# Attention phases that each hold one more pair of score tiles over, with the stack loads awaited at value products and some small work moved to other places

## The chip, the cores and the metric

The kernel runs on one core of a Trainium2 chip. The metric is the device time of one execution in microseconds (us), from three runs of the kernel before: median 1293.32, lowest 1293.25, highest 1293.84. One more execution was taken with the hardware profiler. It took 1295.3 us, of which 1293.3 are the span from the first to the last instruction of the core, and 2.0 lie around the span. All durations below come from that profiled execution.

## What is computed

Two blocks work on the same input `x` (2048 tokens, 512 channels), and a gate mixes them. Cut to what matters:

```python
qkv = x @ wqkv                       # 32 heads of 16 channels
scores = einsum("bhqd,bhkd->bhqk", q, k) * 16 ** -0.5
a = einsum("bhqk,bhkd->bhqd", softmax(scores), v) ... @ wo
h = layernorm(x)
u = gelu(einsum("bsd,sf->bdf", h, w1) + b1)      # mixes along tokens, F = 1792
b = transpose(einsum("bdf,fs->bds", u, w2) + b2)
out = g * a + (1 - g) * b            # g = sigmoid(sum(x * gate_w))
```

Products that need full precision are made of a high and a low part of each factor (three matmuls for one).

## The kernel before, in words

The first 305 us make `v`, `q`, `k` and the first mixer layer. What the change touches is the attention, from 305 us to 1274 us, and a tail of some 20 us behind it.

**Groups and phases.** Attention is cut into 32 groups: 2 halves of the queries by 16 pairs of heads. A group has 4 phases, and the 128 phases are numbered p0 to p127 (p = 4 x group + ph, the loop at L835). In each phase:

- PE (TensorE) makes 16 score tiles of 128x512 (L907) from the group's stacks `ks` (keys) and `qs` (queries). Scores use 64 rows of the array, so that a matmul of the dense work (L916, tile `dn`) runs in the other 64 rows at the same time. The dense work is the second mixer layer in p0 to p91 (14 a phase); there is none in p92 to p95; and it is the output projection in p96 to p127 (12 a phase, then 6, then 8).
- ACT (ScalarE) takes exponentials: six score tiles singly (L928), three pairs of tiles as 128x1024 (L869), and four tiles as one 128x2048 (L939) that DVE (VectorE) has copied out of PSUM before (L924, tile `pe`).
- PE multiplies the exponentials with `v` in `apply_v` (L792): each pair of score tiles takes 8 matmuls of 128x256, in four column groups of 32 that run side by side. They add up in one PSUM bank, `av`, which DVE then copies or adds into the group's sums `ot` in SBUF (L814, L816).

**What a phase holds over.** Two pairs (`HELD`, the four evacuated tiles) are multiplied with `v` one phase later, because their exponential comes last. The last of the other six pairs is held over too where a test in the code allows it (`whole`: both query blocks of a head must be covered, because the sums are kept by column halves). Up to p91 that is so in every phase. In the steady phases from p96 on it fails in half of the phases: there a phase has 56, 64 or 72 value products instead of 64 each.

**Loads and stores.** SP issues DMAs from one queue, in program order. In ph0 of each group it loads the query stacks of the next group (`load_q`, 8 DMAs), in ph1 the key stack (`load_k`, 6 DMAs, L505). The group that has just ended stores its sums in ph0 (8 DMAs: L781 to `o`, L783 to `r`, the sums of exponentials). Nothing waits for the stacks until the next group's first scores use them.

**Turned sums.** After every fourth group, `invert` (L613 to L625) loads `r` (tile `inv`, L617), takes maximum and reciprocal on DVE (L620, L621) and writes it back (L625, `ri`). For the two last blocks of the second half, DVE's part comes in the same phase as the load (p113 and p125), for the others two phases later. `fetch_o` and `fetch_half` (L635 to L650) then load `o` and `ri` again, and DVE multiplies and splits them (L949) for the output projection.

**Order.** The program is written out in the order of each engine; engines run their own instructions in that order. Work that other parts of the kernel want in a phase is put in a table: `call(p, ...)` runs at the start of phase p, ahead of the stack loads of that phase; `on_dve(p, ...)` runs on DVE behind the phase's evacuations and ahead of its sum.

**The tail.** Behind p127, the output projection of the last 8 row tiles is finished on PE: `others` (L996) makes those of the 12 matmuls of each tile that the dense work of the phases has not made.

Of the kernel before, what the change touches and what calls it, by code (L numbers as in the profile page):

```python
# [9 lines left out]
F32 = mybir.dt.float32  # L10
# [5 lines left out]
AX = mybir.AxisListType  # L16
SYNC = mybir.DependencyInfo(mybir.DependencyClass.Sync, mybir.DependencyReason.DATA)
REASON = "the two halves of the rows add to one bank"
PSUM = bass.MemoryType.PSUM
DRAM = bass.MemoryType.DRAM  # L20

P = 128
# [8 lines left out]
NB = 512  # L31
# [27 lines left out]
def gated_mix(ctx: ExitStack, tc: tile.TileContext, a_x, a_wqkv, a_wo, b_w1, b_b1, b_w2, b_b2, gate_w, out):  # L59
# [437 lines left out]


    def stack(dst, src, which, pair, cols, planes):
        b, r0 = divmod(pair * 2 * DH, P)  # L500
        for i in range(2):
            rows = slice(r0 + i * DH, r0 + (i + 1) * DH)
            for row, *part in planes:
                at = slice(i * HALF + row, i * HALF + row + DH)
                nc.sync.dma_start(dst[at].bitcast(F32), src[b][part[which], rows, cols])  # L505

# [58 lines left out]
    def call(at, *what):  # L565
        calls.setdefault(at, []).append(what)
# [14 lines left out]
    def open_end():  # L581

        nonlocal end, sums_of
        u_ctx.close()
        wk_ctx.close()
        end = end_ctx.enter_context(tc.tile_pool(name="end", bufs=1, side="right", reuse_waits="tile"))

        sums_of = end.tile([P, P], F32, name="sums_of")
        nc.vector.tensor_copy(
            sums_of.rearrange("p (j r) -> p j r", r=32),  # L590
            ident.rearrange("p (j r) -> p j r", r=32)[:, :, DH:VC].broadcast_to([P, P // 32, 32]),
        )
        least.append(end.tile([P, 1], F32, name="least"))
# [190 lines left out]

    def apply_v(av, grp, pairs, final=False):

        for n, pair in enumerate(pairs):
            for i, c, qb, pt in sorted(pair, key=lambda u: u[2]):
                for h in range(2):
                    j = 2 * qb + h  # L790
                    v_at = (c * H + grp % NP * 2 + i) * VC
                    nc.tensor.matmul(  # L792
                        av[32 * j : 32 * (j + 1), i * QC : (i + 1) * QC],
                        v_flat[:, v_at : v_at + 32],
                        pt[:, h * QC : (h + 1) * QC],
                        start=n == 0,
                        stop=n == len(pairs) - 1,
                    )
        covered = [{qb for pair in pairs for i, _, qb, _ in pair if i == n} for n in range(2)]
        assert all(len(c) != 1 for c in covered)  # L800
        if grp not in sums:
            sums[grp] = ot_pool.tile([P, NB], F32, name="ot"), [False, False]
        ot, begun = sums[grp]
        halves = [n for n in range(2) if covered[n]]
        if grp == NG - 1 and final:
            parts = [(x, y, True) for x, y in zip(column_halves(ot), column_halves(av))]
        elif len(halves) == 2 and begun[0] == begun[1]:
            parts = [(ot, av, begun[0])]
# [3 lines left out]
        for x, y, more in parts:  # L812
            if more:
                nc.vector.tensor_tensor(x, y, x, ALU.add)  # L814
            else:
                nc.vector.tensor_copy(x, y)  # L816
        for n in halves:
            begun[n] = True
        if final and grp < NG - 1:
            store(grp, sums.pop(grp)[0])  # L820

    engines = {getattr(mybir.EngineType, name) for name in ("PE", "Activation", "DVE", "Pool", "SP")}
    with tc.manual_schedule(engines=engines):
        kt, qt = {0: load_k(0)}, {0: load_q(0)}
        held, fence, turn, spare = [], None, 0, 0

        for n, (step, *args) in enumerate(first):
# [7 lines left out]
        for p in range(LAST + 1):  # L835
            grp, ph = divmod(p, PHASES)
            second = ph % 2
            for what, *args in calls.get(p, ()):
                what(*args)
            if ph == 0:  # L840
                at = [[0, 0], [0, 0]]
                if grp + 1 < NG:
                    qt[grp + 1] = load_q(grp + 1)
            if ph == 1 and grp + 1 < NG:
                kt[grp + 1] = load_k(grp + 1)
            if not second:
                beside = [step(*args) for step, *args in dense.get(p // 2, ())]
# [12 lines left out]

            swap = ph == PHASES - 1 and p < LAST and head[TWO[1][0]] == head[TWO[1][1]]
            order = [*TURNS[:4], TURNS[5], TURNS[4]] if swap else TURNS
# [79 lines left out]
            if p == 0:  # L942
                shift_rows(nc.vector, k_bufs[1])
            if second:
# [7 lines left out]
            spare = share[2]  # L952
            if ph < PHASES - 1 or swap:

                def whole(pairs):
                    met = {(i, qb) for pair in pairs for i, _, qb, _ in pair}
                    return all(len([1 for i, _ in met if i == n]) != 1 for n in range(2))

                if whole(turns[:-1] + (held if ph else [])):
                    now_held = now_held + turns[-1:]  # L960
                    turns = turns[:-1]
            if ph == 0:
                if held:
                    apply_v(av, grp - 1, held, final=True)
                    spare = share[3]
                    av = psum.tile([P, NB], F32, name=f"s{spare}")
                apply_v(av, grp, turns)
            elif p < LAST:
                apply_v(av, grp, held + turns)
            else:  # L970
                ot = sums[grp][0]
# [168 lines left out]
```

## Time and profile before

| what | value |
|---|---|
| median of three runs | 1293.32 us |
| profiled execution / its span | 1295.3 us / 1293.3 us |
| PE busy | 1280.4 us, 99% |
| ACT busy | 1091.3 us, 84% (9 tenths and more in each slice of the attention) |
| DVE busy | 671.0 us, 52% |
| GpSimd (POOL) busy | 180.0 us, 14% |
| granted TensorE clock, mean | 0.997 |
| DMA | 133.20 MB, 101 GB/s of HBM traffic over the span |

A busy PE in this table is one that has matmuls in its pipeline. It is not yet one that could go no faster: the ends of matmuls are modelled, and a matmul that starts late because of a wait is hardly seen in that share. How long a phase takes is better seen from the starts of its weight loads (PEld), which the trace records one by one. The first score of a phase is the first row of L907 behind the last row of L792.

### The profile page before, as it was taken

What the parts mean: (1) busy time and instruction counts of PE and PEld (TensorE: products, weight loads), DVE (VectorE), ACT (ScalarE), POOL (GpSimd) and SP (SyncE); (2) the same over time, 40 slices, a digit from 0 to 9 for tenths busy, and PEclk for the clock granted to TensorE, in tenths of its full rate; (3) what the DMA queues carried; (4) which work ended last, traced back from release to release, by engine and by line L of the source; (5) the groups of instructions that cost most, each with busy time, mean ns of one, the idle gap of its engine ahead of it and who ended that gap; (6) DMA issues with size and microseconds to landing.
All of it is one profiled execution on the core that took longest, in us unless ns stands there. A gap on an engine that the chain in (4) does not pass through costs nothing.

```text
span 1293.3 us, 33067 instructions
## 1 busy us (share of the span) xinstructions
PE 1280.4 (99%) x13278; PEld 850.4 (66%) x13278; DVE 671.0 (52%) x1155; ACT 1091.3 (84%) x1537; POOL 180.0 (14%) x272
## 2 busy tenths in 40 slices
PE   9999999999999999999999999999999999999997
PEld 7888888886666666666666666666665565655555
DVE  5675362438445545544544444454454665645555
ACT  3443343447999999999999999999999999999994
POOL 0210244553110111011011101101110000000000
PEclk9999999999999999999999999999999999999999
DMA  4497643327343343333334443333333654335411
GB/s 131 139 317 276 222 121 98 98 78 159 67 88 75 68 97 83 77 68 81 77 60 98 83 77 66 81 75 60 88 68 75 151 135 114 81 84 108 80 44 72
DMA packets 93581, 133.20 MB, mean 103 GB/s; under 512 B 16277, under 2 KB 55339, under 8 KB 90348
## 3 DMA queue, kind: packets, MB, share of 16 engines
q1 hardware_dynamic: 92844, 129.94, 41.2%
q8 instruction: 108, 1.77, 0.6%
q10 hardware_dynamic: 576, 1.05, 0.2%
q14 instruction: 53, 0.43, 0.1%
HBM read 97.00 MB, written 33.93 MB: 101 GB/s over the span
## 4 chain that ended last, share of the span: by engine, by line
PE 93%; ACT 4%; DVE 1%; issue 1%; DVEq 0%; ACTq 0%
PE av L792 28%; PE s L907 19%; PE acc L416 12%; PE t L907 10%; PE acc L73 10%; PE dn L916 6%; PE s L792 5%; ACT p L928 1%; ACT p L869 1%; ACT pe L939 1%; PE pa L996 1%; DVE pe L924 1%; PE acc L187 1%; PE dn L831 1%; PE acc L254 0%
## 5 line engine op out<-in xcount | busy, mean ns | idle before, releaser
L928 ACT ACTIVATE p<-s 128x512 f32<-128x512 f32 x768 | 395.7, 648 | 6.1 <-PE s L907 3.6
L869 ACT ACTIVATE p<-t 128x1024 f32<-128x1024 f32 x352 | 348.4, 1131 | 0.0
L907 PE MATMUL s<-qs,ks 64*128 64x512 f32 x1344 | 343.0, 404 | 1.1 <-DVE pe L924 0.7
L924 DVE COPY pe<-s 128x512 f32<-128x512 f32 x512 | 317.8, 683 | 6.9 <-PE s L907 6.4
L907 PEld LDWEIGHTS s<-qs,ks 64*128 64x128 f32 x1344 | 232.9, 184 | 97.5 <-issue 52.4
L792 PE MATMUL av<-p,v 128*32 128x256 f32 x4872 | 285.4, 379 | 0.0
L814 DVE TENSOR_TENSOR ot<-av,ot 128x512 f32<-128x512 f32 (+1 forms) x128 | 73.5, 575 | 396.6 <-PE av L792 396.6
L939 ACT ACTIVATE pe<-pe 128x2048 f32<-128x2048 f32 x129 | 259.5, 2014 | 0.0
L792 PEld LDWEIGHTS av<-p,v 128*32 128x32 f32 x4872 | 158.4, 110 | 104.9 <-issue 0.7
L907 PE MATMUL t<-qs,ks 64*128 64x512 f32 x704 | 185.1, 445 | 2.9 <-ACT p L928 0.4
L916 PE MATMUL dn<-u_lo,w_hi 64*128 64x512 f32 x430 | 174.1, 405 | 0.0
L916 PE MATMUL dn<-u_hi,w_lo 64*128 64x512 f32 x430 | 173.9, 404 | 0.0
L916 PE MATMUL dn<-u_hi,w_hi 64*128 64x512 f32 x428 | 173.2, 405 | 0.0
L66 POOL TENSOR_TENSOR w_lo<-w_raw,w_hi 128x512 fp32r<-128x512 f32 (+1 forms) x126 | 149.0, 1189 | 124.6 <-ACT w_hi L65 108.5
L907 PEld LDWEIGHTS t<-qs,ks 64*128 64x128 f32 x704 | 96.2, 184 | 83.4 <-ACT p L928 74.9
L792 PE MATMUL av<-pe,v 128*32 128x256 f32 x2048 | 138.1, 387 | 0.1
L920 POOL MEMSET token<- 1x1 f32 x124 | 12.7, 102 | 866.9 <-PE dn L916 811.2
L65 ACT CAST w_hi<-w_raw 128x512 fp32r<-128x512 f32 (+1 forms) x67 | 38.1, 569 | 79.2 <-PE acc L416 58.8
L792 PEld LDWEIGHTS av<-pe,v 128*32 128x32 f32 x2048 | 53.6, 109 | 54.2 <-ACT p L928 25.3
L416 PE MATMUL acc<-h_hi,w_hi 128*128 128x512 f32 x224 | 87.1, 389 | 0.0
L416 PE MATMUL acc<-h_lo,w_hi 128*128 128x512 f32 x224 | 87.1, 389 | 0.0
L416 PE MATMUL acc<-h_hi,w_lo 128*128 128x512 f32 x224 | 87.1, 389 | 0.0
(151 smaller groups left out, 1507.2 us busy)
## 6 DMA issues: line engine op xcount, KB each, us to landing
w_raw<-in_B_w_dram SPq DMA_DIRECT2D x96, 256.0 KB
ks<-kp SPq DMA_DIRECT2D x192, 128.0 KB
qs<-qp SPq DMA_DIRECT2D x256, 64.0 KB
qp<-pc SPq DMA_DIRECT2D x16, 768.0 KB
x<-in_A_x_dram SPq DMA_DIRECT2D x32, 256.0 KB
kp<-pc SPq DMA_DIRECT2D x16, 512.0 KB
w_raw<-in_B_w_dram SPq DMA_DIRECT2D x32, 128.0 KB
bp<-row SPq DMA_DIRECT2D x16, 256.0 KB
```

The costliest lines, as they stand in the source:

```text
L65: copy(hi, src)
L66: return sub(lo, src, hi.bitcast(F32), ALU.subtract)
L73: nc.tensor.matmul(ps, a, b, start=start and n == 0, stop=stop and n == last)
L416: nc.tensor.matmul(p, a, b, start=first and k == 0, stop=last and k == 2)
L792: nc.tensor.matmul(av[32 * j : 32 * (j + 1), i * QC : (i + 1) * QC], v_flat[:, v_at : v_at + 32], pt[:, h * QC : (h + 1) * QC], start=n == ...
L814: nc.vector.tensor_tensor(x, y, x, ALU.add)
L869: nc.scalar.activation(pt, twos[low, low + 1], AF.Exp, scale=SCALE)
L907: nc.tensor.matmul(s, kt[grp][rows_i, c * P : (c + 1) * P], qt[grp][rows_i, qb * NB : (qb + 1) * NB], start=True, stop=True,)
L916: mm = nc.tensor.matmul(ps, a[half], b[half], start=begin and not second, stop=last and bool(second))
L924: nc.vector.tensor_copy(pt, s)
L928: nc.scalar.activation(pt, s, AF.Exp, scale=SCALE)
L939: nc.scalar.activation(x, x, AF.Exp, scale=SCALE)
```

## The change

1. **Holding over.** Every phase but p127 holds its last pair of scores over. The test `whole` is gone, so that a phase has 64 value products throughout (p0 and p127 apart). For this the sums must be added by quarters: `ot` is set to zero by GpSimd at the start of each group (L844 of the new kernel) and DVE only adds, to the whole bank, to column halves, or to a quarter of 64x256.
2. **Awaiting at products.** `stack` notes each DMA that it issues; the value products of ph3 behind the first pair of tiles each wait for one of them (`await_loads`), in place of the next group's first scores.
3. **Loads ahead.** `load_q` and `load_k` are issued ahead of what the table calls in the same phase: `invert`, `fetch_o`, `fetch_half`, `load_wo`, the rows of `bp`.
4. **Constants and others.** The small constants (`sums_of`, `least`) are made in p101 in place of p92. In p0, the second key buffer's constant rows are set by GpSimd in place of DVE. A subtraction for the output projection moves from p115 to p116. One output tile (the one at p116 and p117) has 6 of its 12 matmuls in the phases in place of 8.

The core of the diff:

```diff
+    landed = []
     def stack(dst, src, which, pair, cols, planes):
...
-                nc.sync.dma_start(dst[at].bitcast(F32), src[b][part[which], rows, cols])
+                landed.append(nc.sync.dma_start(dst[at].bitcast(F32), src[b][part[which], rows, cols]))
...
     call(p0, open_end)
+    on_dve(p0 + 9, end_constants)
...
-    call(p2, fetch_o, 1, 2, (0, 1), (p2 + 1, p2 + 1, p2 + 1))
+    call(p2, fetch_o, 1, 2, (0, 1), (p2 + 1, p2 + 1, p2 + 2))
...
-        at = put_output(t, 6 if 2 * at < p2 + 2 else 8, at)
+        at = put_output(t, 6 if 2 * at < p2 + 3 else 8, at)
...
+                    if await_loads and n and landed:
+                        tc.add_manual_dep(mm.ins, landed.pop(0).ins.name, SYNC, reason=AHEAD_OF_USE)
...
+        if grp == NG - 1 and final:
+            parts = list(zip(column_halves(ot), column_halves(av)))
+        elif len(met) == 4:
+            parts = [(ot, av)]
         else:
-            cols = [slice(n * QC, (n + 1) * QC) for n in range(2)]
-            parts = [(ot[:, cols[n]], av[:, cols[n]], begun[n]) for n in halves]
+            at = [(every, cols[i]) for i in range(2) if {(i, 0), (i, 1)} <= met]
+            at += [(rows[qb], cols[i]) for i, qb in sorted(met) if (i, 1 - qb) not in met]
+            parts = [(ot[r, c], av[r, c]) for r, c in at]
+        for x, y in parts:
+            nc.vector.tensor_tensor(x, y, x, ALU.add)
...
-            for what, *args in calls.get(p, ()):
-                what(*args)
             if ph == 0:
+                sums[grp] = ot_pool.tile([P, NB], F32, name="ot")
+                nc.gpsimd.memset(sums[grp], 0.0)
...
             if ph == 1 and grp + 1 < NG:
                 kt[grp + 1] = load_k(grp + 1)
+            for what, *args in calls.get(p, ()):
+                what(*args)
...
-                shift_rows(nc.vector, k_bufs[1])
+                shift_rows(nc.gpsimd, k_bufs[1])
...
-            if ph < PHASES - 1 or swap:
...
-                if whole(turns[:-1] + (held if ph else [])):
-                    now_held = now_held + turns[-1:]
-                    turns = turns[:-1]
+            if p < LAST:
+                now_held = now_held + turns[-1:]
+                turns = turns[:-1]
...
-                apply_v(av, grp, held + turns)
+                apply_v(av, grp, held + turns, await_loads=ph == PHASES - 1)
```

**PE at the boundary of two groups.** The 15th and 16th score of p20 (tile `t3`, from `qs` and `ks1` of group 5) and the first value products behind them, before:

```order
L907 MATMUL t3_5303<-qs_4740,ks1_2704 128x512 [waits DVE_49,Activation_49]
L907 MATMUL t3_5303<-qs_4740,ks1_2704 128x512 [waits DMAHW6_49,DMAHW5_49,DMAHW4_49]
L792 MATMUL av_5302<-pe_5113,v_91 32x256 [waits Activation_49]
L792 MATMUL av_5302<-pe_5113,v_91 32x256 x7
L792 MATMUL av_5302<-p2_5186,v_91 32x256 x4
```

And now, value products of p19 (from the fifth on), one phase ahead:

```order
L799 MATMUL av_5167<-pe_5001,v_91 32x256 x3
L799 MATMUL av_5167<-pe_5001,v_91 32x256 [waits DMAHW6_49]
L799 MATMUL av_5167<-pe_5001,v_91 32x256 [waits DMAHW7_49]
L799 MATMUL av_5167<-pe_5001,v_91 32x256 [waits DMAHW0_49]
L799 MATMUL av_5167<-pe_5001,v_91 32x256 [waits DMAHW1_49]
L799 MATMUL av_5167<-p2_5074,v_91 32x256 [waits DMAHW2_49]
L799 MATMUL av_5167<-p2_5074,v_91 32x256 [waits DMAHW3_49]
```

The waits for DMA queues (DMAHW) have left the 16th score, which now has none, and fourteen value products of p19 wait for one each (six are shown). An instruction with three waits needs further instructions on PE's sequencer that wait ahead of it; one with a single wait holds it itself.

**SP in p112 and p113 (group 28).** The end of group 27's stores (`o12`, `r12`), the load of the turned sums (`inv`), the next key stack (`ks1`) and the way back (`ri12`), before:

```order
L781 DMA o12_2714<-ot_16057 16x2x256 [waits DMAHW3_49]
L783 DMA r12_2722<-ot_16057 2x1x256 [waits DMAHW4_49]
L617 DMA inv_16520<-r12_2722 128x64 [waits DMAHW5_49,DMAHW4_49,DMAHW6_49,DMAHW2_49,DMAHW0_49]
L505 DMA ks1_2704<-kp3_68 16x2048
L505 DMA ks1_2704<-kp3_68 16x2048 [waits DMAHW7_49]
L505 DMA ks1_2704<-kp3_68 16x2048
L505 DMA ks1_2704<-kp3_68 16x2048 [waits DMAHW1_49]
L505 DMA ks1_2704<-kp3_68 16x2048
L505 DMA ks1_2704<-kp3_68 16x2048 [waits DMAHW3_49]
L625 DMA ri12_2730<-inv_16520 128x64 [waits DVE_49]
```

And now:

```order
L788 DMA o12_2714<-ot_15933 16x2x256 [waits DMAHW3_49]
L790 DMA r12_2722<-ot_15933 2x1x256 [waits DMAHW4_49]
L508 DMA ks1_2704<-kp3_68 16x2048 [waits DMAHW5_49]
L508 DMA ks1_2704<-kp3_68 16x2048 [waits DMAHW6_49]
L508 DMA ks1_2704<-kp3_68 16x2048 [waits DMAHW7_49]
L508 DMA ks1_2704<-kp3_68 16x2048 [waits DMAHW0_49]
L508 DMA ks1_2704<-kp3_68 16x2048 [waits DMAHW1_49]
L508 DMA ks1_2704<-kp3_68 16x2048 [waits DMAHW2_49]
L623 DMA inv_16541<-r12_2722 128x64 [waits DMAHW4_49,DMAHW3_49]
L631 DMA ri12_2730<-inv_16541 128x64 [waits DVE_49]
```

The load of `inv` has gone from ahead of the six key loads to behind them; the write of `ri12` follows it at once.

**DVE in p113 and at the start of p114.** The same instructions stand in the same order before and now. Now (L626 and L627 are the maximum and the reciprocal, L821 the sum of p113, L930 the evacuations of p114):

```order
L930 COPY pe_16543<-s1_16579 128x512 [waits PE_49]
L676 SCALAR_TENSOR_TENSOR base8_16185<-dn_16419,g_77,base8_16185 128x512 [waits DMAHW2_49]
L626 TENSOR_SCALAR inv_16541<-inv_16541 128x64 [waits DMAHW3_49]
L627 RECIPROCAL inv_16541<-inv_16541 128x64 [waits DVE_49]
L821 TENSOR_TENSOR ot_16406<-av_16594,ot_16406 128x512 [waits PE_49]
L930 COPY pe_16657<-s4_16665 128x512 [waits PE_49,Activation_49]
```

Nothing has moved on this engine here. The instruction that waits for `inv` stands ahead of the sum of p113 and of the four evacuations of p114.

More of the change, by code (lines that the diff above doesn't have):

```diff
@@ L17 @@
 SYNC = mybir.DependencyInfo(mybir.DependencyClass.Sync, mybir.DependencyReason.DATA)
+AHEAD_OF_USE = "the next group's scores find their stacks awaited"
 REASON = "the two halves of the rows add to one bank"
@@ L588, in open_end, with end_constants @@
         sums_of = end.tile([P, P], F32, name="sums_of")
+        least.append(end.tile([P, 1], F32, name="least"))
+    def end_constants():
         nc.vector.tensor_copy(
@@ L592, in open_end @@
         )
-        least.append(end.tile([P, 1], F32, name="least"))
         nc.vector.tensor_reduce(least[0], ident.rearrange("p (j r) -> p j r", r=32)[:, :, DH], axis=AX.X, op=ALU.add)
@@ L791, in apply_v @@
                     v_at = (c * H + grp % NP * 2 + i) * VC
-                    nc.tensor.matmul(
+                    mm = nc.tensor.matmul(
                         av[32 * j : 32 * (j + 1), i * QC : (i + 1) * QC],
@@ L825, in gated_mix @@
         held, fence, turn, spare = [], None, 0, 0
+        landed.clear()
         for n, (step, *args) in enumerate(first):
@@ L859, in gated_mix @@
                     turn = 1 - turn
-            swap = ph == PHASES - 1 and p < LAST and head[TWO[1][0]] == head[TWO[1][1]]
+            swap = ph == PHASES - 1 and p < LAST and n_b == NSC - 2
             order = [*TURNS[:4], TURNS[5], TURNS[4]] if swap else TURNS
```

29 lines of the change are left out of this document (7 added, 22 removed).

## The prediction

> **What bounds the kernel now.** I read the page's shares first, then the starts of the phases in the weight loads of the timeline, then the phases that stand out.
>
> ```profile
> PE 1280.4 (99%) x13278; PEld 850.4 (66%) x13278; DVE 671.0 (52%) x1155; ACT 1091.3 (84%) x1537; POOL 180.0 (14%) x272
> ...
> L792 PE MATMUL av<-p,v 128*32 128x256 f32 x4872 | 285.4, 379 | 0.0
> ```
>
> PE seems to be all there is. But the share counts pipelines, and a late matmul hides in it. The rows of the weight loads (start, duration, operation, idle before) tell more. Here are p55 (ph3) and p56 (ph0), from first score to first score, and the six single exponentials of ACT in p55:
>
> ```profile
> 719.37 0.18 PEld L907 LDWEIGHTS s<-qs,ks 64*128 64x128 f32 x1 [0.41 <-issue]
> ...
> 722.81 0.21 PEld L907 LDWEIGHTS t<-qs,ks 64*128 64x128 f32 x2 [0.27 <-ACT p L928]
> 723.27 0.59 PEld L792 LDWEIGHTS av<-pe,v 128*32 128x32 f32 x16 [0.25 <-ACT p L928]
> ...
> 726.86 0.18 PEld L907 LDWEIGHTS s<-qs,ks 64*128 64x128 f32 x1 [0.41 <-issue]
> ...
> 730.31 0.42 PEld L907 LDWEIGHTS t<-qs,ks 64*128 64x128 f32 x2 [0.27 <-ACT p L928]
> 730.97 0.59 PEld L792 LDWEIGHTS av<-pe,v 128*32 128x32 f32 x16 [0.24 <-issue]
> ...
> 734.56 0.18 PEld L907 LDWEIGHTS s<-qs,ks 64*128 64x128 f32 x1 [0.41 <-issue]
> ```
> ```profile
> 719.90 3.09 ACT L928 ACTIVATE p<-s 128x512 f32<-128x512 f32 x6
> ```
>
> p55 takes 726.86 - 719.37 = 7.49 us: 3.90 of scores (to 723.27) and 3.59 of value products. The products start when the sixth single exponential lets a bank go, and the exponentials wait for the scores: PE and ACT bound the phase in one loop. ACT alone has little less to do. Phases without dense work, below, run at 7.39 and 7.40. So nothing large is to be had per phase; the change can only take away excesses over 7.49. p56 has one: its products start 4.11 behind its start, 0.21 late, and the pair of last scores spans 0.42 in place of 0.21.
>
> Now the long stretches: the starts of p4, p92, p93, p94 and p127.
>
> ```profile
> 335.36 0.18 PEld L907 LDWEIGHTS s<-qs,ks 64*128 64x128 f32 x1 [0.41 <-issue]
> ...
> 997.96 0.30 PEld L907 LDWEIGHTS s<-qs,ks 64*128 64x128 f32 x4 [0.41 <-issue]
> ...
> 1007.62 0.30 PEld L907 LDWEIGHTS s<-qs,ks 64*128 64x128 f32 x4 [0.41 <-issue]
> ...
> 1015.01 0.19 PEld L907 LDWEIGHTS s<-qs,ks 64*128 64x128 f32 x2 [0.41 <-issue]
> ...
> 1264.67 0.18 PEld L907 LDWEIGHTS s<-qs,ks 64*128 64x128 f32 x1 [0.41 <-issue]
> ```
>
> **Term 1, stacks awaited at products.** p4 to p91 are 88 phases in 997.96 - 335.36 = 662.60 us; 88 x 7.49 would be 659.12. The excess, 3.5 us, lies in the 22 phases that begin a group, as in p56: the 16th score waits for three or four DMA queues, and each wait beyond those that a matmul can hold is an instruction of its own on PE. Four waits cost 0.21 (p56); for three I estimate half, so 11 x 0.21 + 11 x 0.10 = 3.4. With the waits moved to products of ph3, each holding one, these instructions go: **-3.4**. What the awaited product costs is not seen before, since no product waits for a DMA there. Products that wait for ACT stand in the row of L792 with 0.0 idle: lower end nothing. Upper end: each like one of the waits of its own, 0.21 / 2 = 0.105, times 14 products in 31 groups, 434 x 0.105 = 45.6 us. I take nothing, the row of the same instruction; the data landed many us earlier (loads are issued in ph0 and ph1, awaited in ph3).
>
> **Term 2, p1.** DVE sets constant rows (L492) into p1 and begins the phase's sum late. The starts of p1 and p2, then DVE and ACT:
>
> ```profile
> 312.04 0.18 PEld L907 LDWEIGHTS s<-qs,ks 64*128 64x128 f32 x1 [0.41 <-ACT p L869]
> ...
> 320.38 0.18 PEld L907 LDWEIGHTS s<-qs,ks 64*128 64x128 f32 x1 [0.41 <-issue]
> ```
> ```profile
> 311.60 1.76 DVE L492 MEMSET ks<- 16x2048 f32 x1 [0.46 <-issue]
> 313.40 0.42 DVE L816 COPY ot<-av 128x256 f32<-128x256 f32 x1
> ...
> 313.23 3.09 ACT L928 ACTIVATE p<-s 128x512 f32<-128x512 f32 x6
> ```
>
> p1 takes 8.34; its DVE sum starts 1.36 behind the start, where 0.14 is usual (p114, term 5). So 1.2 of lateness cost 0.85. With GpSimd doing it, ACT remains late: its first exponential is 1.19 behind p1's start, against 0.53 in p55. I keep 0.65 of the 0.85: **-0.2** (-0.85 at the best). GpSimd's memsets, this one and one of 128x512 in each group, lie beside its idle time (14% busy): what uses the result comes half a phase later or more. No row shows them on GpSimd; if a group's first sum did wait, it would be for some part of DVE's 1.76, once a group.
>
> **Term 3, from p92 on.** p92 takes 9.66, because DVE makes the constants ahead of its evacuations, and then the clock falls:
>
> ```profile
> 997.90:1002.30 4.40, 3.69 (x20) 1.66 (x16) 3.60 (x9) 4.40 (x9) 0.00 (x0) 1.00 0.84 196
> 1002.30:1007.60 5.30, 5.30 (x66) 2.44 (x64) 0.42 (x1) 4.01 (x4) 0.00 (x0) 0.68 0.42 87
> ```
>
> (Columns: window, length, busy of PE, weight loads, DVE, ACT, GpSimd, granted clock, DMA share, GB/s.) If the low clock is a half, 0.68 over 5.30 means 3.4 us at half: the 3.59 of products took the 5.3 of this window, 1.7 more. That is a stage with 16 scores and no dense matmuls, prolonged by DVE. Moved to p101, the constants (0.6 us of DVE) lie where DVE, 52% busy, waits for products anyway; without that cover p102 would lose the 0.6. p92 should then look like p93: 1015.01 - 1007.62 = 7.39.
>
> From p95 on, a phase of 72 products is longer by a pair's 3.59 / 8 = 0.45, and one of 56 shorter by as much; but there ACT falls behind, and the next phase gives most of it back. With 64 throughout each phase takes 7.49. So p92 to p126 take 4 x 7.40 + 31 x 7.49 = 261.8, against 1264.67 - 997.96 = 266.7: **-4.9**. This includes the 0.77 that p116 loses before:
>
> ```profile
> 1181.42 0.18 PEld L907 LDWEIGHTS s<-qs,ks 64*128 64x128 f32 x1 [0.41 <-issue]
> ...
> 1189.23 0.18 PEld L907 LDWEIGHTS s<-qs,ks 64*128 64x128 f32 x1 [0.41 <-issue]
> ```
> ```profile
> 1181.28 1.23 DVE L949 TENSOR_TENSOR e<-o_sum,e 128x1024 fp32r<-128x1024 f32 x1
> 1182.42 0.68 DVE L814 TENSOR_TENSOR ot<-av,ot 128x512 f32<-128x512 f32 x1
> ```
>
> p116 has 56 products and should take 7.49 - 0.45 = 7.04; it takes 7.81. DVE's sum, 0.86 later than usual, holds the evacuations behind it and the scores that need their banks. The subtraction of 1.23 now comes a phase later. So a late sum costs a phase its lateness less 0.1 to 0.35 (0.86 gives 0.77, 1.2 gives 0.85).
>
> **Term 4, the tail.** One tile leaves two more matmuls to L996, behind p127, where PE alone sets the end:
>
> ```profile
> 1274.08 0.39 PE L996 MATMUL pa<-wo_lo,e 128*128 128x512 f32 x1
> 1274.31 0.39 PE L996 MATMUL pa<-wo_hi,e 128*128 128x512 f32 x1
> ```
>
> One each 0.23: **+0.5**.
>
> **Term 5, p113.** The load of `inv` goes behind the six key loads, and DVE waits for it ahead of the phase's sum. SP before (the first row is the last store), the starts of p113 and p114, DVE, and the same load at p125, where no key loads are:
>
> ```profile
> 1160.20 0.57 SPq L783 DMA_DIRECT2D r<-ot  x1
> 1161.96 0.34 SPq L617 DMA_DIRECT2D inv<-r  x1
> 1162.35 3.51 SPq L505 DMA_DIRECT2D ks<-kp  x6
> 1165.90 0.42 SPq L625 DMA_DIRECT2D ri<-inv  x1
> ...
> 1171.14 0.63 SPq L636 DMA_DIRECT2D o_sum<-ri  x1
> ```
> ```profile
> 1158.24 0.18 PEld L907 LDWEIGHTS s<-qs,ks 64*128 64x128 f32 x1 [0.41 <-issue]
> ...
> 1166.01 0.18 PEld L907 LDWEIGHTS s<-qs,ks 64*128 64x128 f32 x1 [0.41 <-issue]
> ```
> ```profile
> 1164.84 0.20 DVE L620 TENSOR_SCALAR inv<-inv 128x64 f32<-128x64 f32 x1 [2.63 <-DMA inv<-r]
> 1165.07 0.55 DVE L621 RECIPROCAL inv<-inv 128x64 f32<-128x64 f32 x1
> 1166.15 0.69 DVE L814 TENSOR_TENSOR ot<-av,ot 128x512 f32<-128x512 f32 x1 [0.53 <-PE av L792]
> ```
> ```profile
> 1253.13 0.32 SPq L617 DMA_DIRECT2D inv<-r  x1
> ```
> ```profile
> 1254.77 0.19 DVE L620 TENSOR_SCALAR inv<-inv 96x64 f32<-96x64 f32 x1 [1.38 <-DMA inv<-r]
> ```
>
> Times from p113's start: the stores end at 1160.77 - 1158.24 = 2.5; now 2.1 to 2.5, as p112 has 64 products and ends 0.4 later. Six key loads of 3.5 follow at once, so `inv` is issued at 5.6 to 6.0 (before: 3.7). How long is it on its way? 1.6 at p125, 2.9 here before (1161.96 to 1164.84), 5.2 for the small `ri` right behind the six key loads (1165.90 to 1171.14, when its reader could be issued). Maximum and reciprocal take 0.8. The sum then starts at 8.0 to 8.4, 9.3 to 9.7, or 11.6 to 12.0. It is due 0.14 into p114, at 7.6. So it is late by 0.6, 1.9 or 4.2. The nearest row is that of `ri`, but its writing ends in another memory than the load of `inv`; I take the middle of the two upper ones, 3.1, which costs 2.9. While p114's scores stand still PE has as little to do as in p92, and the clock may fall again and cost 1.7; I add 1.3, three quarters. **+4.2**, with bounds 0.3 and 4.1 + 1.7 = 5.8. What waits behind DVE's waiting instruction are the sum, four evacuations, and so half of p114's scores.
>
> The Trainium skill bears on both steps, in two sentences that may be left out. DMA: Bandwidth & Descriptors (Queues, rings and completion order) says that SP's DMAs share one ring on each engine and are taken in ring order, so that `inv` would wait for all key packets: by it, the lateness is 4.2 and the sum -2.7 in place of -3.8 (the row of `ri` agrees, that of p125 has no loads ahead). TensorE: Matmul & The Clock Gate (Part 1) says that the clock goes to half after an idle window of about 3.4 us; the 3.4 us at half in p92 agree, and by it p114 would lose the whole 1.7 or nothing, for a sum of -3.4 or -5.1.
>
> **Sum.** -3.4 - 0.2 - 4.9 + 0.5 + 4.2 = -3.8, on the profiled execution of 1295.3 (span 1293.3 and 2.0 around it). That stands 2.0 above the median of 1293.3; the same difference put to the median gives 1289.5. The rest of the change lies beside idle time: the added quarter sum (64x256) runs behind held products, in mid-phase, where DVE waits (without that cover at most the 0.42 of the 128x256 form at 313.40, in 8 groups: 3.4); other loads that now go behind stack loads are read a phase or more later.
>
> **Rivals.**
> - **No stall in p114.** `inv` lands 1.6 us after its issue, as at p125: 0.6 late, 0.4 lost. The sum is -8.0 + 0.4 = -7.6: 1285.7. Against it speaks `ri`'s 5.2 behind the same loads; for it, that keys and `inv` are issued over 3.5 us, in which most key bytes may have moved.
> - **The awaited products cost PE time** (slower). The place is ph3 of 31 groups, the price 434 times x. At x = 3.8 / 434 = 9 ns all gain is gone; at 15 ns, 1296; at the upper end of 105 ns, 1335. For it: products go four side by side about every 0.2 us, so PE may stand for its sequencer. Against: 0.0 idle for the products that wait for ACT.
> - **The excess of p56 stays.** The first score or another instruction takes over its late part, so that term 1 is nothing: 1292.9.
>
> **How the numbers follow.** The forecast (all gains, a stall of 2 to 6 in p114): 0.58, from 1287.3 to 1291.1. No stall: 0.19. Awaited products: 0.11. The excess stays or the change does not do what it says: 0.12. A measurement of this kernel can tell 0.2% (2.6 us) from no change. Faster by more than that, below 1290.7: 0.45 of the forecast's 0.58 and all of the no-stall case, 0.64. Within: 0.13 of the forecast and most of the last case, 0.24. Slower: 0.12. The range takes in both faster cases with their bounds and most of the last, 1284.8 to 1292.9.
>
> **What would show it.** Term 1: the two last scores of ph0 span 0.21 in every group, and ph0 takes 7.49. Term 3: p92 at 7.4 with the clock at 1.00, and p96 to p126 at 7.49 each. Term 5: `inv` issued behind `ks`, DVE idle for it in p113, the sum late, and p114 at 9.5 to 13 us. The prediction is wrong if p114 is below 8 (1285.7), or if ph3 is longer than 7.49 (products that pay for waits), or if p92 still falls to half clock.

## The result and the profile after

| | kernel before | changed kernel |
|---|---|---|
| median of 12 runs | 1293.60 us | 1294.29 us |
| lowest, highest | 1292.34, 1297.15 | 1293.41, 1295.39 |
| profiled execution, span | 1295.3, 1293.3 | 1294.68, 1292.5 |

The ratio is 1.0001, with a 95% interval of 0.9992 to 1.001: no difference that can be measured (the two medians differ by 0.7 us, which lies within the interval). Two executions that stand far from all others, 2478 us of a6_eight and 7006 us of the kernel before, are left out of the medians below. Faster was forecast, 1289.5, and the range of 1284.8 to 1292.9 does not hold the result. Yet inside the span much has moved. The phases' starts, read as in the prediction, give this table (us; "rest" is what lies behind p127's last product; term 3's forecast is split by its 4 x 7.40 and 31 x 7.49):

| stretch | before | after | difference | forecast |
|---|---|---|---|---|
| start of p0 | 304.7 | 304.4 | -0.3 | 0 |
| p0 to p3 | 30.7 | 29.8 | -0.9 | -0.2 |
| p4 to p91 | 662.6 | 659.6 | -3.0 | -3.4 |
| p92 to p95 | 32.3 | 30.0 | -2.4 | -2.7 |
| p96 to p126 without p114 | 226.9 | 225.6 | -1.3 | -2.2 |
| p114 | 7.5 | 14.3 | +6.8 | +4.2 |
| p127 and rest | 28.6 | 28.9 | +0.3 | +0.5 |

**The gains came.** The page still shows a PE that is busy all the time:

```profile
PE 1275.1 (99%) x13276; PEld 838.4 (65%) x13276; DVE 671.4 (52%) x1142; ACT 1088.5 (84%) x1537; POOL 198.0 (15%) x306
...
L799 PE MATMUL av<-p,v 128*32 128x256 f32 x4904 | 289.5, 380 | 0.0
```

Weight loads at p56, the first phase of a group, then the starts of p57, p4, p92, p93, p94 and p127:

```profile
723.94 0.18 PEld L913 LDWEIGHTS s<-qs,ks 64*128 64x128 f32 x1 [0.41 <-issue]
...
727.38 0.21 PEld L913 LDWEIGHTS t<-qs,ks 64*128 64x128 f32 x2 [0.25 <-ACT p L934]
727.84 0.59 PEld L799 LDWEIGHTS av<-pe,v 128*32 128x32 f32 x16 [0.25 <-ACT p L934]
...
731.43 0.18 PEld L913 LDWEIGHTS s<-qs,ks 64*128 64x128 f32 x1 [0.41 <-issue]
```
```profile
334.17 0.18 PEld L913 LDWEIGHTS s<-qs,ks 64*128 64x128 f32 x1 [0.41 <-issue]
...
993.77 0.30 PEld L913 LDWEIGHTS s<-qs,ks 64*128 64x128 f32 x4 [0.41 <-issue]
...
1001.24 0.19 PEld L913 LDWEIGHTS s<-qs,ks 64*128 64x128 f32 x2 [0.41 <-issue]
...
1008.78 0.30 PEld L913 LDWEIGHTS s<-qs,ks 64*128 64x128 f32 x4 [0.41 <-issue]
...
1263.57 0.18 PEld L913 LDWEIGHTS s<-qs,ks 64*128 64x128 f32 x1 [0.41 <-issue]
```

p56's two last scores span 0.21 where they spanned 0.42, its products start 3.90 behind the phase's start where it was 4.11, and it takes 7.49. The trace also counts the instructions by which PE's sequencer only waits: 566 before, 427 now. The awaited products cost nothing that shows in their own phase: the row of L799 still has 0.0 idle, and phases of ph3 have 7.48 to 7.50. p92 takes 7.47, at full clock.

**One phase took them back.** SP, DVE, PE and ACT in p113 and p114, and the starts of p114 and p115:

```profile
1154.59 2.71 SPq L508 DMA_DIRECT2D ks<-kp  x6
1157.40 0.37 SPq L623 DMA_DIRECT2D inv<-r  x1
1164.19 0.34 SPq L631 DMA_DIRECT2D ri<-inv  x1
```
```profile
1163.38 0.20 DVE L626 TENSOR_SCALAR inv<-inv 128x64 f32<-128x64 f32 x1 [7.38 <-DMA inv<-r]
1163.61 0.55 DVE L627 RECIPROCAL inv<-inv 128x64 f32<-128x64 f32 x1
1164.08 0.63 DVE L821 TENSOR_TENSOR ot<-av,ot 128x512 f32<-128x512 f32 x1
1164.62 2.47 DVE L930 COPY pe<-s 128x512 f32<-128x512 f32 x4
```
```profile
1164.76 1.12 PE L913 MATMUL s<-qs,ks 64*128 64x512 f32 x4 [3.58 <-DVE ot L821]
```
```profile
1160.10 1.59 ACT L934 ACTIVATE p<-s 128x512 f32<-128x512 f32 x3
1165.35 1.70 ACT L934 ACTIVATE p<-s 128x512 f32<-128x512 f32 x3 [3.65 <-PE s L913]
```
```profile
1159.50 0.18 PEld L913 LDWEIGHTS s<-qs,ks 64*128 64x128 f32 x1 [0.41 <-issue]
...
1173.77 0.18 PEld L913 LDWEIGHTS s<-qs,ks 64*128 64x128 f32 x1 [0.41 <-issue]
```

`inv` is issued at 1157.40 and can be used at 1163.38: 6.0 us on its way. The trace records the packets in which a DMA moves its bytes, and they tell where these 6.0 us go. The 96 packets of the six key loads (8 KB each) start between 1155.91 and 1160.49; the 128 packets of `inv` (256 bytes each) start between 1161.10 and 1161.96. So 3.7 us pass from the issue to the first packet, while key packets move. Before, with no keys ahead, it was 0.97 (1161.96 to 1162.93).

DVE stands idle for 7.38 us. Its sum begins at 1164.08. It was due 0.14 behind p114's start of 1159.50, at 1159.64, so it is 4.4 late. The evacuations stand behind it, the scores that need their banks behind them (PE idle for 3.58 us), and ACT is idle for 3.65. Then the clock falls. The windows of p114 (length, busy of PE, weight loads, DVE, ACT, GpSimd, granted clock, DMA share, GB/s):

```profile
1159.50:1165.60 6.10, 2.42 (x20) 1.42 (x16) 2.19 (x5) 2.45 (x5) 0.09 (x1) 1.00 0.32 36
1165.60:1172.60 7.00, 6.83 (x55) 3.12 (x57) 1.49 (x3) 5.97 (x7) 0.00 (x0) 0.51 0.62 167
```

7.0 us at 0.51: the products of p114 start 8.46 behind its start, where 3.89 is usual, and take 5.82, where 3.59 is usual. So p114 loses 4.6 in the scores and 2.2 in the products.

### The profile page after: what moved, and what is told of

Its sections match the earlier page's. It is cut to its first block, busy times and chain, and to the rows that moved or that the text cites. A ratio compares the mean times of both kernels' runs of the same rounds, so it can differ in the third digit from the quotient of the medians.

```text
span 1292.5 us, 33044 instructions
## 1 busy us (share of the span) xinstructions
PE 1275.1 (99%) x13276; PEld 838.4 (65%) x13276; DVE 671.4 (52%) x1142; ACT 1088.5 (84%) x1537; POOL 198.0 (15%) x306
## 4 chain that ended last, share of the span: by engine, by line
PE 88%; ACT 9%; issue 1%; DVE 1%; SPq 0%; DMA 0%; ACTq 0%
PE av L799 27%; PE s L913 20%; PE acc L417 12%; PE t L913 11%; PE acc L74 10%; PE s L799 4%; ACT p L934 3%; ACT p L875 3%; ACT pe L945 2%; PE dn L922 2%; PE pa L996 1%; PE acc L188 1%; PE dn L835 1%; PE acc L255 0%; DMA inv<-r 0%
## 5 line engine op out<-in xcount | busy, mean ns | idle before, releaser
L934 ACT ACTIVATE p<-s 128x512 f32<-128x512 f32 x768 | 413.2, 783 | 8.1 <-PE s L913 7.8
L875 ACT ACTIVATE p<-t 128x1024 f32<-128x1024 f32 x352 | 365.6, 1264 | 0.0
L913 PE MATMUL s<-qs,ks 64*128 64x512 f32 x1344 | 339.1, 403 | 4.2 <-DVE ot L821 3.6
L930 DVE COPY pe<-s 128x512 f32<-128x512 f32 x512 | 317.8, 682 | 5.6 <-PE s L913 4.9
L799 PE MATMUL av<-p,v 128*32 128x256 f32 x4904 | 289.5, 380 | 0.0
L821 DVE TENSOR_TENSOR ot<-av,ot 128x512 f32<-128x512 f32 (+2 forms) x137 | 83.3, 609 | 393.0 <-PE av L799 392.8
L945 ACT ACTIVATE pe<-pe 128x2048 f32<-128x2048 f32 x129 | 276.8, 2148 | 0.0
L799 PEld LDWEIGHTS av<-p,v 128*32 128x32 f32 x4904 | 159.8, 110 | 106.6 <-issue 2.0
L913 PE MATMUL t<-qs,ks 64*128 64x512 f32 x704 | 180.2, 451 | 4.5 <-DVE pe L930 0.3
L913 PEld LDWEIGHTS t<-qs,ks 64*128 64x128 f32 x704 | 89.5, 185 | 91.5 <-ACT p L934 89.9
L799 PE MATMUL av<-pe,v 128*32 128x256 f32 x2048 | 138.1, 387 | 0.0
L799 PEld LDWEIGHTS av<-pe,v 128*32 128x32 f32 x2048 | 53.6, 109 | 55.2 <-ACT p L934 31.3
```

Source lines behind the costliest of these rows:

```text
L799: mm = nc.tensor.matmul(av[32 * j : 32 * (j + 1), i * QC : (i + 1) * QC], v_flat[:, v_at : v_at + 32], pt[:, h * QC : (h + 1) * QC], start ...
L875: nc.scalar.activation(pt, twos[low, low + 1], AF.Exp, scale=SCALE)
L913: nc.tensor.matmul(s, kt[grp][rows_i, c * P : (c + 1) * P], qt[grp][rows_i, qb * NB : (qb + 1) * NB], start=True, stop=True,)
L930: nc.vector.tensor_copy(pt, s)
L934: nc.scalar.activation(pt, s, AF.Exp, scale=SCALE)
L945: nc.scalar.activation(x, x, AF.Exp, scale=SCALE)
```

## The experiments

Names with a or d are variants of the changed kernel, b of the kernel before, and c is a copy of the latter. Each was compared with runs of the kernel before on the same chip. There were three such comparisons, each on another chip: a1, a2, a3 and b1; a5, a9, b2 and c1; a6, a8 and d1. Between comparisons only the ratios can be set side by side. What is said of single phases is read from one profiled execution of each.

### The load ahead of the keys again: a1_inv_first

```diff
+            for what, *args in calls.get(p, ()):
+                if what is invert:
+                    what(*args)
             if ph == 1 and grp + 1 < NG:
                 kt[grp + 1] = load_k(grp + 1)
             for what, *args in calls.get(p, ()):
-                what(*args)
+                if what is not invert:
+                    what(*args)
```

> The changed kernel, but the load of the turned sums (inv) is again issued ahead of the key loads of its phase; nothing else is different. Theory 1 (the gains came and the stall of p114 gave them back): p114 falls from 14.27 to 7.5 us, the clock stays at 1.00 there, and the kernel is 6.8 us faster than the changed one: 1287.5, a ratio of 0.995 to the kernel before. Theory 2 (the stall is DVE's wait for a transfer that is slow there anyway, whatever stands ahead of it): p114 stays above 10 us and the ratio stays at 1.000. Theory 3 (the stall costs what the trace shows, but the gains were smaller in ordinary runs than between the two profiles): p114 is 7.5, and the ratio is above 0.997.

Measured: 1288.9 us, ratio 0.9968 (0.9956 to 0.9981). Its DVE in p113, and the starts of p114 and p115:

```profile
1157.63 0.20 DVE L626 TENSOR_SCALAR inv<-inv 128x64 f32<-128x64 f32 x1 [1.45 <-DMA inv<-r]
...
1159.82 0.69 DVE L821 TENSOR_TENSOR ot<-av,ot 128x512 f32<-128x512 f32 x1 [1.41 <-PE av L799]
```
```profile
1159.68 0.18 PEld L917 LDWEIGHTS s<-qs,ks 64*128 64x128 f32 x1 [0.41 <-issue]
...
1167.16 0.18 PEld L917 LDWEIGHTS s<-qs,ks 64*128 64x128 f32 x1 [0.41 <-issue]
```

The sum again waits for PE, 0.14 behind the phase's start, and p114 takes 7.48. From p0 on all other stretches are those of the changed kernel within 0.1 us, and the span is 1286.0, 6.5 less. Theory 2 falls. The ratio, 0.9968, lies between theories 1 and 3: its interval reaches into theory 3's range, above 0.997, and ends short of theory 1's 0.995. The run with a copy of the kernel before, below, bears on why it is not 0.995.

### The load behind the keys alone: b1_inv_behind

```diff
             for what, *args in calls.get(p, ()):
-                what(*args)
+                if what is not invert:
+                    what(*args)
...
                 kt[grp + 1] = load_k(grp + 1)
+            for what, *args in calls.get(p, ()):
+                if what is invert:
+                    what(*args)
```

> The kernel before, with only the load of the turned sums put behind the key loads of its phase (at all eight places). Theory 1: this alone makes a stall of some 4.5 us in p114's scores and a clock fall behind it: 6 to 7 us slower than before, 1300, a ratio of 1.005. Theory 2 (the stall needs the rest of the change): no difference, ratio 1.000.

Measured: 1298.37 us, ratio 1.0039 (1.0025 to 1.0053). Its SP and DVE:

```profile
1159.86 2.72 SPq L505 DMA_DIRECT2D ks<-kp  x6
1162.67 1.76 SPq L617 DMA_DIRECT2D inv<-r  x1
```
```profile
1168.71 0.20 DVE L620 TENSOR_SCALAR inv<-inv 128x64 f32<-128x64 f32 x1 [7.46 <-DMA inv<-r]
```

p114 takes 12.73 in place of 7.48, with one stretch of 3.41 us at half clock behind its late scores. The same place, the same wait of DVE, without anything else of the change: this one move costs 5 us by itself. That is less than the 6 to 7 of theory 1; the half clock is half as long here as in the changed kernel.

### How many keys ahead: a5_inv_mid

The load of `inv` is issued behind the first three of the six key loads (`load_k` calls `invert` between its two halves).

> The changed kernel, with the load of the turned sums between the third and the fourth key load of its phase. Theory 1 (the small load lands when the bytes of the key loads that are issued ahead of it have moved): inv lands some 3 us sooner than behind six, p113's sum is 1 to 2.5 us late in place of 4.4, and p114 takes 8.5 to 10. Rival (any load ahead holds it, by the wait for room or by the engine): p114 stays at 12 to 14 us. Rival (only the place behind all six hurts, as then the next loads follow): p114 at 7.5.

Measured: 1290.15 us, ratio 0.9971 (0.9961 to 0.9982).

```profile
1155.32 1.37 SPq L510 DMA_DIRECT2D ks<-kp  x3
1156.80 0.36 SPq L625 DMA_DIRECT2D inv<-r  x1
```
```profile
1161.13 0.20 DVE L628 TENSOR_SCALAR inv<-inv 128x64 f32<-128x64 f32 x1 [4.41 <-DMA inv<-r]
```

4.3 us on its way, against 6.0 behind six. The sum is 1.5 late, and p114 takes 10.15, a little above the 10 that theory 1 gave. So in the profiles the loss goes with the number of key loads ahead: p114 takes 7.5, 10.2 and 14.3 us for none, three and six. The time from the issue of `inv` to its first packet goes the same way: 1.0 us in the profile of each variant that has no keys ahead, 1.5 here, and 3.3 to 3.7 behind six (the changed kernel, b1_inv_behind, d1_turn_later). The medians do not show the step from none to three: the ratio is that of a1_inv_first within the noise, and the profiled execution, 1291.37 us, is the slowest of the seven.

### Another queue: a9_pool_queue

```diff
-        nc.sync.dma_start(t, r_d[half][k][:n]...)
+        (nc.gpsimd if (half, k) == (1, 2) else nc.sync).dma_start(t, r_d[half][k][:n]...)
```

> The changed kernel, key loads ahead as in it, but p113's load of the turned sums is issued from GpSimd's queue. Theory 1 (inv is late because it stands in one queue behind the keys): it is issued when r has landed, about 3 us sooner, takes its turn among the key packets, and p113's sum is in time or up to 1 us late: p114 at 7.5 to 8.5, and the kernel 5 to 6.8 us faster than the changed one. Rival (the DMA engines are simply full of key bytes, and any load started then waits): p113's sum is 2 us late or more and p114 above 9.5.

Measured: 1293.13 us, ratio 0.9992 (0.9983 to 1.0001).

```profile
1156.77 0.68 POOL L623 DMA_DIRECT2D inv<-r  x1 [9.83 <-PE t L913]
```
```profile
1163.32 0.20 DVE L626 TENSOR_SCALAR inv<-inv 128x64 f32<-128x64 f32 x1 [6.81 <-DMA inv<-r]
```

Counted from p114's start (1160.02 here), the issue is 1.2 us sooner than in the changed kernel, but the way is 6.5 us, and p114 takes 12.95. The sum is 3.9 late. Theory 1's sizes fail, and the rival's, 2 us late or more and p114 above 9.5, hold. The packets show a part of it: `inv` now moves as 16 packets of 2 KB, which start between 1160.22 and 1160.79, among key packets that run to 1162.07. So it does not stand behind all the keys, but its first packet comes 3.45 us after the issue. From GpSimd's queue the same load was not run without keys, so this may be that queue's own time, or the engines' being full of key bytes. What is settled is that GpSimd's queue is no way out here.

### The order on DVE: d1_turn_later

```diff
-            call(p0, invert, half, k, pairs, p0 + (0 if half and k > 1 else 2))
+            call(p0, invert, half, k, pairs, p0 + ((2, 2, 1, 0)[k] if half else 2))
...
-    call(p2, fetch_o, 1, 2, (0, 1), (p2 + 1, p2 + 1, p2 + 2))
+    call(p2 + 1, fetch_o, 1, 2, (0, 1), (p2 + 3, p2 + 3, p2 + 4))
```

> The changed kernel with the key loads ahead as they are, but DVE takes the turn of the sums loaded in p113 one phase later (behind p114's evacuations), and what uses it follows two phases later than in the changed kernel. Theory 1 (the order on DVE makes the loss: a wait of 4.4 us ahead of the sum): p114 takes 7.5 although inv lands as late as before, and the kernel is 6.8 us faster than the changed one, as a1_inv_first is or up to 0.5 better, since it has no wait left there. Rival (late turned sums are needed soon in any case): the stall moves to p117 or p118, and the gain is below 3 us.

Measured: 1288.69 us, ratio 0.9963 (0.9949 to 0.9976). DVE in p114:

```profile
1161.23 2.48 DVE L930 COPY pe<-s 128x512 f32<-128x512 f32 x4
1163.95 0.20 DVE L626 TENSOR_SCALAR inv<-inv 128x64 f32<-128x64 f32 x1 [0.23 <-DMA inv<-r]
```

`inv` lands almost as late as in the changed kernel (3.55 us behind p114's start, where it was 3.88), but the four evacuations have been done, and DVE waits 0.23 us. p114 takes 7.48 and no later phase is longer. So the late load is no harm by itself: the loss is made by what stands behind the waiting instruction on DVE. The ratios of this version and of a1_inv_first lie below those of both kernels; between the two no run tells a difference.

### The awaited products: a2_no_await

As a1_inv_first, with `await_loads=False`.

> As a1_inv_first, and no value product awaits a DMA, so that the next group's scores wait for the stacks as they did before. Theory 1: the first phase of each group from p4 to p88 goes back from 7.49 to 7.6 or 7.7, 3.0 us in all, so 1290.5 if a1_inv_first is at 1287.5. Rival (the awaited products cost what they save, and the gain of p4 to p91 came from the loads being issued ahead): p4 to p91 keep 659.6 us, and the time is that of a1_inv_first within 0.5 us.

Measured: 1291.02 us, ratio 0.9983 (0.9974 to 0.9992): 2.1 us slower than a1_inv_first. p4 to p91 take 661.94, 2.3 more than with the awaits, where theory 1 had 3.0 and the rival nothing. PE's waiting instructions go from 427 back to 553. The mean of ph0 there goes from 7.49 back to 7.63, but that of ph1 falls from 7.53 to 7.49. So the awaits bring 0.14 in a group's first phase and lose 0.04 in its second; why is left open. The other 0.7 us between 661.94 and the 662.6 of before came from the rest of the change; which part of it was not tried.

In this run `inv`, although ahead of the keys, was 3.9 us on its way, and p114 took 7.96. Its first packet comes 1.0 us after the issue, as in a1_inv_first; the 2.2 more lie behind that:

```profile
1158.42 0.34 SPq L623 DMA_DIRECT2D inv<-r  x1
```
```profile
1162.29 0.19 DVE L626 TENSOR_SCALAR inv<-inv 128x64 f32<-128x64 f32 x1 [3.59 <-DMA inv<-r]
```

### The holding over: a3_whole

As a1_inv_first, with the test `whole` of the kernel before.

> As a1_inv_first, but a phase holds its last pair over only where it did before (56, 64 or 72 value products in the phases from p95 on); the sums still start from zero. Theory 1 (even phases bring about 0.28 us a group, but the first sum of each group has become 0.25 longer in p97 to p109, which takes most of it back): 1 us slower than a1_inv_first. Rival (even phases bring what the forecast gave them, some 0.3 to 0.4 in each of 8 groups): 2.5 to 3 us slower.

Measured: 1289.91 us, ratio 0.9975 (0.9966 to 0.9985): 1.0 us slower than a1_inv_first, as theory 1 has it. Up to p112 even phases bring nothing: p96 to p112 take 127.93 without and 128.31 with them. They bring 0.4 in p95 and 1.2 from p113 to p126; what they bring between goes into p97, p101, p105 and p109, which take 7.74 with them (a8_noquarter tells why).

### The quarter sum: a8_noquarter

```diff
-            at += [(rows[qb], cols[i]) for i, qb in sorted(met) if (i, 1 - qb) not in met]
+            if final:
+                at += [(rows[qb], cols[i]) for i, qb in sorted(met) if (i, 1 - qb) not in met]
```

> As a1_inv_first, but the quarter sums of the first phase of each group are left out (part of the sums is missing, for the time alone). Theory Q (the 0.25 by which p97, p101, p105 and p109 are long comes from the second piece of DVE's first sum, 0.17, and its later start): these four phases fall from 7.74 to 7.5 and the kernel gains 1.0 us over a1_inv_first. Rival (the order of the dense matmuls or of ACT makes them long): they stay at 7.74.

Measured: 1288.01 us, ratio 0.9955 (0.9941 to 0.997). DVE at the start of p97 in the changed kernel, and in this one:

```profile
1031.42 0.86 DVE L821 TENSOR_TENSOR ot<-s,ot 128x256 f32<-128x256 f32 x2 [1.33 <-issue]
```
```profile
1032.22 0.42 DVE L822 TENSOR_TENSOR ot<-s,ot 128x256 f32<-128x256 f32 x1 [1.33 <-issue]
```

p97, p101, p105 and p109 take 7.51 to 7.53 in place of 7.74. The first sum of a group, cut into two pieces of 0.43, makes DVE late at the start of the next phase, and 0.22 of it come out each time: 0.9 in four phases, as theory Q has it. The time does not show it: in this profile p116 takes 8.16 in place of 7.48 (there DVE waited for a load of `o_sum` and made its sum 0.8 late), so that the span is no shorter than that of a1_inv_first, and the ratios of the two overlap.

### The tail: a6_eight

As a1_inv_first, with 8 in place of 6 matmuls at p116 and p117 (`6 if 2 * at < p2 + 2 else 8`).

> As a1_inv_first (inv ahead of the keys), and the output tile of p116 and p117 has 8 of its matmuls in the phases again in place of 6, so that two matmuls leave the tail. Forecast's step: 2 x 0.23 = 0.46 us faster than a1_inv_first, 1288.4 where that was 1288.9; the stretch behind p127 shrinks from 19.96 to 19.5. Rival (the two matmuls lie beside other waits in the tail): no difference.

Measured: 1288.42 us, ratio 0.9959 (0.9945 to 0.9972). The stretch from p127's start on is 0.23 shorter than in a1_inv_first, half of the 0.46, but in the profiles of the other variants of the changed kernel it takes anything from 28.7 to 29.4 us (28.83 here), so that 0.23 tells nothing. p126 is 0.23 longer, since `inv` of p125 was 3.4 us on its way in place of 1.7. The step of 0.46 is neither confirmed nor refuted.

### The kernel before once more, and the constants alone: c1_before, b2_constants

> The kernel before once more, unchanged, for a second profile. Theory A (the forecast was made against an unusual execution: p92's fall of the clock, 1.7 us, is in a minority of executions): a profiled execution near the median, at most 1293.8, shows p92's products at 3.59 and the clock at 1.00 there, so that p92 takes about 8 us; the mean clock of the timed runs is 0.998 or 0.999 in most. Theory B (the clock falls in p92 in every execution): p92 takes 9.6 again, with 3.4 us at half clock.

> The kernel before, with only the constants made in p101 in place of p92. Theory A: p92 takes 7.4 to 7.5, and as its clock falls only in a minority of executions before, the median gains the late scores alone, 0.5 us (ratio 0.9996). Theory B: the median gains 2.2 us (ratio 0.9983).

The second holds the change's `end_constants` in p101 and nothing else of it. Measured: the copy 1293.86 us, ratio 1.0002 (0.9994 to 1.0011); constants alone 1293.16, ratio 0.9995 (0.9986 to 1.0004). The stretch from p92's products on, in the copy and with the constants moved:

```profile
1002.50:1007.80 5.30, 5.30 (x66) 2.64 (x64) 0.43 (x1) 4.00 (x4) 0.00 (x0) 0.68 0.35 92
```
```profile
1002.50:1007.80 5.30, 5.29 (x70) 2.80 (x62) 2.45 (x5) 5.30 (x8) 0.00 (x0) 1.00 0.42 94
```

The copy's profile shows the fall in p92 too, in an execution of 1295.98 us, far above its median, so theory A's own test was not met: no profile without the fall was caught. What speaks for A are the timed runs, of which only the mean clock is known. Of the 32 runs of the kernel before in this comparison, 9 had 0.997, with spans of 1292.2 to 1293.4; 23 had 0.998 or 0.999, with spans of 1290.0 to 1292.1. Of the copy's 12, five had 0.997 or less beside the profiled one. With the constants moved, none of 11 was below 0.998, and no span above 1291.8. The mean clock is a rough sign, since the end of each profiled span is at half clock too, for 1.5 to 5.1 us. With such an end, 0.997 needs some 3.4 us more at half clock, as in p92, 0.999 has no room for them, and 0.998 fits both. Of the 23, 9 had 0.999 and 14 had 0.998, and the spans of these 14 are no longer than those of the 9. The moving takes 2.3 us off p92 in the profile (9.67 to 7.39), but 0.4 off the median (0.7 against the copy), where theory A gave 0.5 and theory B 2.2. So the fall of p92 is in a minority of executions: argued from the clocks and the medians, not seen.

## Why the prediction was wrong

**Term 1, right.** -3.0 against -3.4. The instructions that waited are gone, and the awaited products cost nothing in their own phase; their rival is refuted (it needed 9 ns for each, which would be 0.13 us in each ph3). The 22 phases of ph0 gained 3.8, a little more than forecast, and the 0.04 in each ph1 took 0.9 back.

**Term 2, right in kind.** p1 fell from 8.33 to 8.19, near the 0.2 of the forecast. The rest of the 0.9 by which p0 to p3 are shorter is p0: 7.35 before, 6.58 after. The copy of the kernel before has 7.29 there, b1_inv_behind and b2_constants, where nothing of p0 had been changed, have 6.57, and the variants of the changed kernel 6.56 to 7.20. So it can't be put down to the change; what makes it was not tried.

**Term 3, right in its places, too large.** p92 and p116 fell to 7.47 and 7.48. p97, p101, p105 and p109 stayed 0.25 above 7.49: the quarter sum that was said to run in mid-phase is in truth two, one of them in the first sum of the group, and that one stands at the head of DVE's work of the next phase. That is 1.0 of the missing 1.2. The prediction had put this sum at nothing.

**Term 4, not told.** +0.3 on p127 and the rest, but the same stretch takes 28.4 to 29.0 in four profiles of kernels in which it had not been changed (before, the copy, b1_inv_behind, b2_constants).

**Term 5, the step that failed.** The mechanism was as forecast: `inv` behind the keys, DVE idle for it, the sum late, p114's scores held, the clock falling behind them. The term was mis-sized: +6.8 in place of +4.2, beyond its upper bound of 5.8. Its time on the way was taken from the middle of 2.9 and 5.2, and it was 6.0; the sum's lateness, 4.4, cost 4.6 in the scores, not 0.2 less (in a5_inv_mid, b1_inv_behind and a9_pool_queue too the scores lose the lateness and 0.1 more); and the clock stayed low for 6.8 us, twice the 3.4 of p92, so that the products lost 2.2 and not 1.3. The upper of the two rows, `ri` behind six key loads, was the one like it, as the prediction itself said, and it was averaged with one that had no key loads ahead. The rule that the Trainium skill gives in DMA: Bandwidth & Descriptors (Queues, rings and completion order), one ring for SP's DMAs on each engine, taken in ring order, would have given the higher value. The packets agree with it: 1.0, 1.5 and 3.7 us to the first one for none, three and six key loads ahead. a2_no_await's 3.9 us with no key ahead shows that it is not the whole of the way.

**The carry to the median, wrong.** On the two profiles the change gained 0.6 us (1295.3 to 1294.68), where 3.8 was forecast; on the medians it lost 0.7, which is not clear of noise. So of the 4.8 us between the forecast and the result 3.2 are seen in the profiles, term 5's 2.6 the largest part, and 1.6 come from the carry. The forecast was made on a profiled execution that held p92's fall of the clock, and the saving was put to the median as it stood. If the fall is in a third of the executions, as the clocks of before let one think, some 1.1 of term 3's 4.9 is no gain for the mean. The changed kernel's executions are not alike either: their mean clock is 0.996 in the five longest (the profiled one of 1294.68 among them), but 0.998 in three of 1293.4 to 1293.8, so that p114's fall need not be 6.8 us in each. This is argued, not seen. It may also be part of why a1_inv_first, 7.0 us faster than before by the two profiled executions, is only 4.1 faster by the medians; the 0.8 of p0 may be another.

## What to carry to other kernels

A small load that a busy engine waits for belongs ahead of bulk loads on its queue, or its use belongs behind the work that others wait for on that engine: either alone brought 4 to 5 us here. When a load is put behind others, take its time from a row where the same load, or one like it, stood behind the same others, and count what stands behind the waiting instruction. And before a saving read in one profiled execution is put to a median, ask whether the event that it removes is in every execution: spans and mean clocks of the other runs tell.

## What the runs showed of the hardware that was not expected

- A late stage can cost twice, and the second cost does not follow the length of the first. In p114, PE stood for 3.6 us in the changed kernel, 3.0 in a9_pool_queue, 3.4 in b1_inv_behind and 0.6 in a5_inv_mid; then the clock was at a half for 6.8, 6.8, 3.4 and 3.4 us. In the traces, each of these stretches, and that of p92 in the kernel before, begins a whole number of 3.413 us steps (292 to 342 of them) behind the first record of full clock. In the step ahead of each, PE was busy for 0.8 to 2.7 us, so no whole step of idling is needed. The place of a stall among these steps may decide how many it costs; that was not tried.
- A load of 32 KB (`inv`) was on its way for 1.7 us (a1_inv_first) and 3.9 (a2_no_await) with the key loads issued right behind it, in the same place of the program. The 24 KB load at p125, with no key loads, took 1.6 to 3.4 us over the profiles, though its first packet always came 0.95 after the issue. A margin of one us is none.
- With the awaits at the products, ACT's instructions are recorded some 0.14 us longer, though they start at the same distances (the three in a phase 0.90 us apart in both kernels). The groups of pairs of tiles, with awaits (the changed kernel) and without (a2_no_await):

```profile
L875 ACT ACTIVATE p<-t 128x1024 f32<-128x1024 f32 x352 | 365.6, 1264 | 0.0
```
```profile
L879 ACT ACTIVATE p<-t 128x1024 f32<-128x1024 f32 x352 | 347.8, 1124 | 0.0
```

So a longer mean of an engine's records is no sign by itself that its work takes longer; the distance of starts is. What makes the record longer was not tried.
